# A fused attention and Fourier-mixing kernel: mirrored rows of batch 2 computed on chip again, the last batch's turned in DRAM in four column pieces

## The chip, the core and the metric

The kernel runs on one core of one Trainium2 chip. The core has five engines with instruction queues of their own: TensorE (PE in the profile, its weight loads PEld), VectorE (DVE), ScalarE (ACT), GpSimd (POOL) and SyncE (SP). SP and ACT also issue most of the DMA transfers. The metric is the device time of one execution in microseconds (us); lower is better. Times of engines below are counted from the start of the profiled span.

## What is computed

The inputs are q, k, v of shape (4 batches, 8 heads, 768 positions, 64) and two matrices of an MLP. Attention looks at 8 global positions and at a local band of 96, with a bias per head; its output x has shape (4, 768, 512). Then follows a Fourier mixing and an MLP:

```
scores = q k^T / sqrt(D) + bias, masked; a = softmax(scores); x = a v, as (B, 768, 512)
X     = fft(fft(x, axis=1), axis=2)
u     = x + real(X)
un    = (u - mean(u)) / sqrt(var(u) + 1e-6)
out   = u + max(un @ w_ch1, 0) @ w_ch2
```

For real x the real part of the two-dimensional transform is symmetric: the value at row -s, column -d equals the value at row s, column d. Rows s = 6m+1 and 6m+2 therefore hold, in reverse order of rows and of columns, what is needed for rows 6m+5 and 6m+4.

## The kernel before, in words

Work is written for one batch at a time: attention (scores `score`, P·V `av`), then `bounce`, `fold_s`, `fold_d`, `y_unit`, `mirror`, `u_unit`, `nt_unit`, and then the MLP (`ph_unit` for the first matrix, `pg_unit` and, for the last pair, `pg_last` for the second). The 768 rows of a batch are six residue classes 6m+r of 128 rows. They are handled as three pairs of classes; pair number c = 3b + pr runs from 0 to 11 over the whole kernel.

- `bounce` writes the attention output X to a DRAM buffer (xd, L737) and reads it back by residue class (xr; L751 and L752, and L760 for the classes 4 and 5). From batch 1 on it issues all this on ACT.
- `fold_s`, `fold_d` and `y_unit` make the first transform by foldings on DVE and matmuls on PE (py, L934 to L941). ACT or DVE empty PSUM into Y (tile zy, L955 and L957). Only 14 of the 24 combinations of row and column class are computed; the others are mirror images.
- `u_unit` makes the second transform of a pair by 16 matmuls (pu, L1032); `u_rows` adds x on DVE (L1072).
- `nt_unit` normalises and transposes. For b > 1 the transposes are DMA transposes on SP (L1121); each call of the function `xbar` there issues two, one for each class of the pair.
- `ph_unit` (L1171, emptied by ACT L1177 or DVE L1178) and `pg_unit` (L1194, the sum with u on DVE L1205, the store L1216) finish a pair. The output tile ob has two buffers. The last half pair is made in two column halves, with the add at L1243 and the store at L1246.

There are two ways to the mirrored classes 4 and 5. `FLIP(b)` chooses; it is true for batches 2 and 3.

1. Without FLIP (batches 0 and 1), `mirror` makes reversed copies of Y (r0 for one tile, and rn, L993, for four more in a tile of tag ww), and the pairs are (1,2), (0,3), (4,5): three u units.
2. With FLIP, only r0 is done. The pair (1,2) and the pair (5,4) share one PSUM bank of one u unit: the second is read backwards in columns (`turned` in `u_rows`). Its rows are in reverse order too. So x of these classes is turned in DRAM: two DRAM-to-DRAM transfers into xe (L757), then one read into SBUF (xr from xe, L764). And its output is stored to a staging buffer in DRAM (oe, L1214) and from there, turned, into the output (`back`, L1221). The turning transfers run over 16 column pieces, then rows, then the elements of a piece. This makes two u units a batch.

The order of instructions comes from a planner, `Plan`. Every piece of work has an assumed cost and the tokens it needs. Matmuls stand in four streams (MIX, ATT, PH, PG), of which the first ready one is taken; the rest of the engines get what is ready earliest. Nothing at run time reorders an engine's queue. Work that gets its engine late holds all behind it on that engine. The planner's figures for DMA (for example 1.35 us of ACT for all of `rd`) are constants in the code.

A buffer is reused when its users are done: `buf(tag, i, ..., users)` sets the number of users and `pl.used` counts them. Tag ww has one buffer.

The main loop, at its end, for one batch (the branch for FLIP ends with `continue`):

```python
mirror(b)
if FLIP(b):
    nt_unit(b, 0)
    nt_unit(b, 1)
    u_unit(b, 2)
    nt_unit(b, 2)
    continue
if b:
    u_unit(b, 0)
u_unit(b, 1)
for rows in ((0,), (1,)):
    nt_unit(b, 0, rows)
u_unit(b, 2)
nt_unit(b, 1)
nt_unit(b, 2)
```

Of the kernel before, what the change touches and what calls it, by code (L numbers as in the profile page):

```python
# [9 lines left out]
FP16 = mybir.dt.float16  # L10
# [4 lines left out]
P = 128  # L15
# [139 lines left out]
def mm_us(n, k=1):  # L155
    return k * max(n / 2400.0 + 0.0025, 0.029)


def act(n):
    return 0.19 + n / 1200.0  # L160
# [15 lines left out]
def kernel(  # L176
# [11 lines left out]
    nc = tc.nc  # L188
    B, H, S, Dh = q.shape
# [92 lines left out]
    def free(tag, i):  # L282
        i -= NBUF[tag]
        return [("free", tag, i)] if i >= 0 else []

    def buf(tag, i, shape, dtype, users):
        pl.users(("free", tag, i), users)
        return wk.tile(shape, dtype, tag=tag, name=f"{tag}_{i}", bufs=NBUF[tag])
# [18 lines left out]
    v16 = [kon.tile([P, NS, H, 66], FP16, tag=f"v16{i}", name=f"v16{i}") for i in range(2)]  # L307
# [181 lines left out]
    def BANKS(b):  # L489
        return ("xx", "C", "D") if b == 0 else ("xx",)  # L490
# [234 lines left out]
    T = {}  # L725

    def bounce(b):

        on, eng = ("ACT", nc.scalar) if b else ("SP", nc.sync)
        for half in range(2):  # L730
            def wr(half=half):
                if half == 0:
                    XD[b] = dr.tile([S, Dm], FP16, tag="xd", name=f"xd_{b}", bufs=2)
                c = slice(half * 256, half * 256 + 256)
                rows = XD[b][:, c].rearrange("(j m t) d -> t m j d", t=2, m=64)
                for t in range(2):
                    eng.dma_start(rows[t], X[b][64 * t:64 * t + 64, :, c])  # L737
            pl.later([(on, 1.2, wr)], [("x", b, hp, jp) for hp in (2 * half, 2 * half + 1) for jp in range(NP)] + [("xwi", b)][:half], 0.0,
                     [("xw", b, half)], [("free", "x", b)], lat=4.4 if b == 1 else 1.6, dma=1.2,
                     then=lambda t, half=half: half or pl.tok.__setitem__(("xwi", b), pl.t[on]))  # L740

        XE = {}

        def issued(t):
            pl.tok[("xri", b)] = pl.t[on]
            pl.tok[("xe", b)] = t + 4.0

        def rd():
            rows = XD[b].rearrange("(m r) d -> m r d", r=6)
            XR[b] = [buf(f"xr{i}", b, [P, 2, DP if i == 1 and FLIP(b) else Dm], FP16, 1) for i in range(3)]  # L750
            eng.dma_start(XR[b][0], rows[:, 1:3])  # L751
            eng.dma_start(XR[b][2 if FLIP(b) else 1], rows[:, 0:4:3])  # L752
            if FLIP(b):

                XE[0] = dr.tile([2, P, Dm], FP16, tag="xe", name=f"xe_{b}", bufs=2)
                for a in range(2):
                    eng.dma_start(XE[0][a].rearrange("m (h d) -> h m d", h=16),  # L757
                                  rows[::-1, 4 + a].rearrange("m (h d) -> h m d", h=16))
            else:
                eng.dma_start(XR[b][2], rows[:, 4:6])  # L760
        pl.later([(on, 1.35, rd)], [("xw", b, 0), ("xw", b, 1)] + free("xr0", b) + free("xr1", b) + free("xr2", b), 0.0,
                 [("xr", b)], lat=2.0 if b else 0.6, dma=2.2, then=issued)
        if FLIP(b):
            pl.later([(on, 0.5, lambda: eng.dma_start(XR[b][1][:, :, 0:Dm], XE[0].rearrange("a p d -> p a d")))], [("xe", b)], 0.0,  # L764
                     [("xrb", b)], lat=2.0, dma=0.7)
# [73 lines left out]
    def NA(b):  # L839
        return (0, 2, 1, 1)[b]  # L840

    def IW(b, n):

        return (0, 2, 6, 8)[b] + n
# [125 lines left out]
    def mirror(b):  # L970

        def r0(cp):
            rev = buf("rev0", b, [P, 2, 2, P], FP16, 2)
            src = T[("y", b)][:, 4]
            cp(rev[:, 0, :, 0:1], src[:, 0, :, 0:1])
            cp(rev[:, 0, :, 1:P], src[:, 0, :, P - 1:0:-1])
            cp(rev[:, 1], src[:, 1, :, ::-1])
            Y[(b, 0, 3, "r")], Y[(b, 3, 3, "r")] = rev[:, 0], rev[:, 1]
        pl.later([("ACT", 1.0, lambda: r0(nc.scalar.copy)), ("DVE", 0.8, lambda: r0(V.tensor_copy))] if b else
                 [("POOL", 1.0, lambda: r0(nc.gpsimd.tensor_copy))], [("y", b, 0, 3), ("y", b, 3, 3)] + free("rev0", b), 0.0,  # L980
                 [("y", b, 0, 3, "r"), ("y", b, 3, 3, "r")], [("free", "zy", 2 * b + 1)])
        if FLIP(b):
            return

        def rn(n, on):
            if n == 0:
                T[("rev", b)] = buf("ww", IW(b, NA(b) + 1), [P, 4, 2, 2, P], FP16, 1)
            rev = T[("rev", b)]
            d, y = rev[:, n], T[("y", b)][:, n, :, :, ::-1]
            if on == "ACT":  # L990
                A(d, y, AF.Copy)
            else:
                (V if on == "DVE" else nc.gpsimd).tensor_copy(d, y)  # L993
            for a in range(2):
                Y[(b,) + YG[n // 2][2 * (n % 2) + a] + ("r",)] = rev[:, n, a]
        for n in range(4):
            ys = YG[n // 2][2 * (n % 2):2 * (n % 2) + 2]
            pl.later([("ACT", act(512), lambda n=n: rn(n, "ACT")), ("DVE", 0.7, lambda n=n: rn(n, "DVE")) if b else ("POOL", 1.0, lambda n=n: rn(n, "POOL"))],
                     [("y", b) + y for y in ys] + free("ww", IW(b, NA(b) + 1)) + [("rv", b, n - 1)][:n], 0.0,
                     [("y", b) + y + ("r",) for y in ys] + [("rv", b, n)],  # L1000
                     [("free", "zy", 2 * b + 1)] if n == 3 else [])

    def ysrc(rs, rd):
        if (rs, rd) in POS:
            return rs, rd, False
        return (6 - rs) % 6, 4 - rd if rd else 0, True
# [1 line left out]


    def FLIP(b):  # L1010
        return b > 1

    def PAIRS(b):
        return ((1, 2), (5, 4), (0, 3)) if FLIP(b) else ((1, 2), (0, 3), (4, 5))
# [7 lines left out]
    def u_unit(b, pr):  # L1022
        src = {(a, rd): ysrc(rs, rd) for a, rs in enumerate(PAIRS(b)[pr]) for rd in range(4)}
        needs = [("y", b, r2, d2) + (("r",) if m else ()) for r2, d2, m in src.values()]

        def run(start, ring):
            pu = bank(ring, f"pu_{NP * b + pr}")
            for (a, rd), (r2, d2, mir) in src.items():
                yy = Y[(b, r2, d2, "r") if mir else (b, r2, d2)]
                o = pu[:, a, rd * P:(rd + 1) * P]  # L1030
                for x in range(2):
                    nc.tensor.matmul(o, yy[:, x, :], t2_sb[:, rd, (0 if x == 0 else (2 if mir else 1)), :],  # L1032
                                     start=(x == 0), stop=(x == 1))
            e = pl.pe(mm_us(P, 16), start)
            if pr < 2 or FLIP(b):
                pl.used(("free", "zy", 2 * b + 1), e)
            if PAIRS(b)[pr] == (0, 3):
                for _ in range(2):
                    pl.used(("free", "rev0", b), e)
                if not FLIP(b):  # L1040
                    for _ in range(3):
                        pl.used(("free", "zy", 2 * b + 1), e)
            if PAIRS(b)[pr] == (4, 5):
                pl.used(("free", "ww", IW(b, NA(b) + 1)), e)
            if FLIP(b) and pr == 0:
                u_rows(NP * b, pu, e, None)
                u_rows(NP * b + 1, pu, e, ring)
            else:
                u_rows(NP * b + pr, pu, e, ring)
        MIX.append((needs + ([("h", 0, 1)] if b == 0 and pr == 2 else []), BANKS(b) if pr < 1 else ("xx",), run))  # L1050
# [133 lines left out]
    def pg_unit(c, t, part):  # L1184
        b, pr = divmod(c, NP)
# [3 lines left out]
        def run(start, ring):  # L1189
# [11 lines left out]
            cell = {}  # L1201
# [7 lines left out]
            eng = nc.scalar if c < 6 else nc.sync  # L1209
# [8 lines left out]

            def back():
                o = out[b].rearrange("(m r) d -> m r d", r=6)[::-1, rs, :]  # L1220
                eng.dma_start(o.rearrange("m (h d) -> h m d", h=16), cell[1].rearrange("m (h d) -> h m d", h=16))  # L1221
            if FLIP(b) and pr == 1:
                pl.later([("ACT" if c < 6 else "SP", 0.45, back)], [("st", i)], 0.0, [], lat=1.6, dma=1.0)
        PG.append((needs, ("pg",) if part == 0 else None, run))
# [29 lines left out]
    with tc.manual_schedule():  # L1254
# [79 lines left out]
        for b in range(B):  # L1334
# [39 lines left out]
            for g in (0, 1, 2, 3):  # L1374
# [4 lines left out]
                if FLIP(b) and g == 1:  # L1379
# [4 lines that stand above are left out]
# [58 lines left out]
```

## Time and profile before

| | |
|---|---|
| five runs, us | 268.36, 269.26, 271.26, 271.51, 274.1; median 271.26 |
| profiled execution, us | 271.26 |
| its span from first to last instruction, us | 269.5 |
| mean granted clock of TensorE | 0.994 |
| DMA packets, of these under 512 bytes | 100302, 62388 |
| DMA moved | 42.81 MB, 159 GB/s over the span |
| xe from xd: issues, KB each, median us to landing | 4, 128.0, 5.4 |
| oe from ob | 4, 256.0, 2.0 |
| out from oe (turned store) | 4, 256.0, 3.5 |
| DMA transposes of un (L1121): issues, us to landing | 12, 2.5 |

How to read the profile: an engine's busy time is the time its instructions ran; idle time is put down to the work that ended it. A name with q (ACTq, SPq) is the engine's instruction queue at work on something that is not counted as busy, such as issuing a transfer; "issue" is waiting that the profile can't attribute. DMA share is the mean busy share of the 16 DMA engines in a window; records of packets overlap, so it can exceed 1. The granted clock is the share of TensorE's full clock that it was given.

### The profile page before, as it was taken

Reading aid. Unit: us, or ns where it says so; the run is one execution under the profiler, and the core shown is the slowest. Engines: PE = TensorE matmul, PEld = TensorE weight load, DVE = VectorE, ACT = ScalarE, POOL = GpSimd, SP = SyncE. Lnnn points to the kernel's source line nnn. Section 1 sums busy time; section 2 is a strip of 40 time slices with the busy share of each in tenths; the row PEclk is TensorE's granted clock in tenths of the full one; section 3 lists DMA queues with packets and bytes.
Section 4 is the critical chain, followed back from the end, with each engine's and each line's share of the span. In section 5 each row is a group of like instructions: output and inputs, shape, how many; then the busy total and the mean of one; then the engine's idle time right before and its main releaser. Section 6 shows DMA issues by size and latency. Waiting matters only on the chain.

```text
span 269.5 us, 5931 instructions
## 1 busy us (share of the span) xinstructions
PE 255.2 (95%) x2378; PEld 172.2 (64%) x2378; DVE 179.3 (67%) x367; ACT 135.7 (50%) x231; POOL 67.9 (25%) x120
## 2 busy tenths in 40 slices
PE   7789898999999999999998799999999999999993
PEld 3445587887765466877964456677676676666453
DVE  4676978867789998968796478779956614211221
ACT  2877366878633758686331337782353353524000
POOL 1573624597111452534031301011000110100000
PEclk9999999999999999999999799999999999999999
DMA  7999979999989979997299932022572442411144
GB/s 217 291 295 301 201 197 227 219 262 208 214 203 297 314 231 206 208 170 114 61 182 198 235 86 71 4 41 58 129 126 61 120 96 60 98 39 41 39 117 117
DMA packets 100302, 42.81 MB, mean 159 GB/s; under 512 B 62388, under 2 KB 96180, under 8 KB 100148
## 3 DMA queue, kind: packets, MB, share of 16 engines
q1 hardware_dynamic: 79332, 29.86, 48.6%
q10 hardware_dynamic: 16720, 8.39, 12.7%
q0 software_dynamic: 4224, 4.19, 9.7%
q8 instruction: 18, 0.29, 0.5%
q14 instruction: 8, 0.07, 0.1%
HBM read 34.05 MB, written 11.01 MB: 167 GB/s over the span
## 4 chain that ended last, share of the span: by engine, by line
PE 75%; DMA 9%; DVE 6%; ACTq 3%; SPq 2%; POOL 1%; issue 1%; ACT 1%; DVEq 0%; POOLq 0%
PE ph L1171 29%; PE pg L1194 27%; PE sc L569 4%; PE pu L1032 3%; PE pav L698 3%; DMA xe<-xd 2%; DMA qs<-in_q_dram 2%; PE pt L531 2%; SPq L405 2%; DMA qkT<-qk 2%; PE py L934 2%; DVE x L718 2%; PE py L938 2%; DMA out_dram<-ob 1%; DMA xd<-x 1%
## 5 line engine op out<-in xcount | busy, mean ns | idle before, releaser
L1171 PE MATMUL ph<-unT,w 128*128 128x256 f16 x768 | 94.0, 273 | 0.4 <-ACT hT L1177 0.2
L1194 PE MATMUL pg<-w,hT 128*128 128x512 f16 x368 | 87.1, 382 | 0.0
L1171 PEld LDWEIGHTS <-w 128*128 128x128 f16 x768 | 72.1, 98 | 16.8 <-issue 5.3
L1177 ACT ACTIVATE hT<-ph 128x512 f16<-128x512 f32 x59 | 35.0, 596 | 51.7 <-PE ph L1171 42.2
L1194 PEld LDWEIGHTS <-hT 128*128 128x128 f16 x368 | 35.0, 98 | 36.1 <-issue 2.0
L592 ACT ACTIVATE er<-sc 128x992 f16<-128x992 f32 (+2 forms) x42 | 38.0, 924 | 9.7 <-PE sc L569 6.0
L1205 DVE SCALAR_TENSOR_TENSOR ob<-pg,sm,u 128x512 f32<-128x512 f32 x23 | 17.2, 748 | 38.2 <-PE pg L1194 32.9
L1178 DVE TENSOR_SCALAR hT<-ph 128x512 f16<-128x512 f32 x37 | 25.4, 688 | 16.6 <-PE ph L1171 16.2
L607 DVE TENSOR_TENSOR ex<-er,mk 128x992 f16<-128x992 f16 (+2 forms) x42 | 28.2, 689 | 2.3 <-ACT er L592 2.2
L423 POOL CAST qk<-qs 128x768 f16<-128x768 f32 x21 | 19.1, 914 | 25.0 <-issue 12.2
L1110 POOL TENSOR_SCALAR sm<-sm 128x2 f32<-128x2 f32 x12 | 3.0, 249 | 82.6 <-ACT un L1103 82.5
L718 DVE TENSOR_TENSOR x<-pav,rc 128x512 f16<-128x512 f32 (+1 forms) x27 | 17.1, 632 | 0.9
L1072 DVE SCALAR_TENSOR_TENSOR u<-pu,xr 128x512 f32<-128x512 f32 x24 | 15.7, 688 | 2.3 <-PE pu L1032 1.8
L1103 ACT ACTIVATE un<-un 128x512 f16<-128x512 f16 x24 | 15.0, 624 | 4.4 <-DMA unT<-un 3.4
L569 PE MATMUL sc<-qkT 64*128 64x256 f16 (+1 forms) x192 | 16.1, 261 | 0.7 <-ACT v L470 0.5
L698 PEld LDWEIGHTS <-ex 128*128 128x128 f16 x352 | 15.1, 97 | 2.0 <-DVE rc L717 0.4
L698 PE MATMUL pav<-v,ex 128*128 128x65 f16 x352 | 16.3, 193 | 0.0
L955 ACT ACTIVATE zy<-py 128x512 f16<-128x512 f32 x17 | 9.8, 594 | 12.4 <-DVE eA L873 5.2
L479 POOL CAST v<-vs 128x768 f16<-128x768 f32 x12 | 11.6, 977 | 12.1 <-DMA vs<-in_v_dram 11.9
L512 POOL COPY kG<-qkT 64x8 f16<-64x8 f16 x32 | 8.0, 251 | 25.5 <-DVE qkT L540 18.7
L330 PE MATMUL fill<-eg 128*128 128x512 f16 x46 | 12.6, 419 | 1.4 <-DVE eg L1268 1.2
L569 PEld LDWEIGHTS <-qkT 64*128 64x128 f16 x192 | 6.3, 94 | 11.7 <-issue 9.0
(120 smaller groups left out, 285.5 us busy)
## 6 DMA issues: line engine op xcount, KB each, us to landing
vs<-in_v_dram SPq DMA_DIRECT2D x24, 192.0 KB, 5.5
w<-in_moe_w_ch_dram POOLq DMA_DIRECT2D x8, 512.0 KB, 9.7
qs<-in_q_dram SPq DMA_DIRECT2D x9, 384.0 KB, 6.5
qs<-in_k_dram SPq DMA_DIRECT2D x9, 384.0 KB, 5.9
out_dram<-ob ACTq DMA_DIRECT2D x12, 256.0 KB, 4.0
xd<-x ACTq DMA_DIRECT2D x12, 192.0 KB, 3.5
xr<-xd ACTq DMA_DIRECT2D x7, 256.0 KB, 4.9
out_dram<-ob SPq DMA_DIRECT2D x7, 256.0 KB, 2.1
```

Of the source, the lines that this page charges most:

```text
L423: nc.gpsimd.tensor_copy(d, s)
L569: nc.tensor.matmul(pa[:, s, c0:c0 + cw], TT[n][lo:lo + 64, 1, i * P:(i + 1) * P], TT[n][lo:lo + 64, 0, i * P:i * P + cw], start=(not inps) ...
L592: A(mine(), cut(pa), AF.Exp, 0.0, 0.125)
L607: VT(o, mine(), m, op=ALU.mult)
L698: nc.tensor.matmul(po[:, jj, hh * 65:(hh + 1) * 65], lhsT, v16[b % 2][:, i, h, 0:65], start=(jp == 0 and a == 0), stop=(a == len(ops) - 1) ...
L718: VT(X[b][:, 2 * jp:2 * jp + 2, first * Dh:(first + nh) * Dh].rearrange("p j (h d) -> p j h d", d=Dh), pv[:, :, :, 0:Dh], rc.to_broadcast( ...
L1072: V.scalar_tensor_tensor(o.rearrange("p (n r) -> p n r", r=4), i, 1.0, xx.rearrange("p (n r) -> p n r", r=4), op0=ALU.mult, op1=ALU.add, a ...
L1171: nc.tensor.matmul(ph[:, a * CH:(a + 1) * CH], w1[:, d, jb * P:(jb + 1) * P], UNT[c][:, d, :], start=(d == 0), stop=(d == ND - 1))
L1177: pl.later([("ACT", act(512), lambda: A(dst, ph, AF.Relu)), ("DVE", dve(512), lambda: V.tensor_scalar_max(dst, ph, 0.0))], [], e, [("h", c ...
L1178: ("DVE", dve(512), lambda: V.tensor_scalar_max(dst, ph, 0.0))],
L1194: nc.tensor.matmul(pg, HT[c][:, jb, t * P:(t + 1) * P], w2[:, jb, :], start=(jb == 0), stop=(jb == NJ - 1))
L1205: V.scalar_tensor_tensor(cell[0], pg, MV[c][:, t, 3:4], UT[c][:, t, 0:Dm], op0=ALU.mult, op1=ALU.add)
```

## The change

`FLIP` becomes true for the last batch alone, so batch 2 takes the first way: four more reversed copies of Y, the pairs (1,2), (0,3), (4,5), three u units, a plain read of x for classes 4 and 5, plain stores, and the other branch of the main loop, with its two calls of `nt_unit` for the first pair. Its reversed copies lie in v16[0], the tile of V of batches 0 and 2, once batch 2's P·V is done (`avdone`). In the last batch the turning transfers run over 4 column pieces in place of 16 (256 bytes at a time in place of 64 for xe, 512 in place of 128 for the output), and xe is issued on SP in place of ACT.

```diff
                 for a in range(2):
-                    eng.dma_start(XE[0][a].rearrange("m (h d) -> h m d", h=16),
-                                  rows[::-1, 4 + a].rearrange("m (h d) -> h m d", h=16))
+                    nc.sync.dma_start(XE[0][a].rearrange("m (h d) -> h m d", h=4),
+                                  rows[::-1, 4 + a].rearrange("m (h d) -> h m d", h=4))
...
             if n == 0:
-                T[("rev", b)] = buf("ww", IW(b, NA(b) + 1), [P, 4, 2, 2, P], FP16, 1)
+                if b < 2:
+                    T[("rev", b)] = buf("ww", IW(b, NA(b) + 1), [P, 4, 2, 2, P], FP16, 1)
+                else:
+                    T[("rev", b)] = v16[0].rearrange("p j h d -> p (j h d)")[:, 0:16 * P].rearrange(
+                        "p (n a c m) -> p n a c m", n=4, a=2, c=2)
...
-                     [("y", b) + y for y in ys] + free("ww", IW(b, NA(b) + 1)) + [("rv", b, n - 1)][:n], 0.0,
+                     [("y", b) + y for y in ys] + (free("ww", IW(b, NA(b) + 1)) if b < 2 else [("avdone", b)]) + [("rv", b, n - 1)][:n], 0.0,
...
     def FLIP(b):
-        return b > 1
+        return b == B - 1
...
-            if PAIRS(b)[pr] == (4, 5):
+            if PAIRS(b)[pr] == (4, 5) and b < 2:
                 pl.used(("free", "ww", IW(b, NA(b) + 1)), e)
...
-                eng.dma_start(o.rearrange("m (h d) -> h m d", h=16), cell[1].rearrange("m (h d) -> h m d", h=16))
+                eng.dma_start(o.rearrange("m (h d) -> h m d", h=4), cell[1].rearrange("m (h d) -> h m d", h=4))
```

## The prediction

> **What bounds the kernel now.** I read the page's busy shares first, then who waited for whom on PE, then the chain of waits and ACT's timeline around PE's one long hole, then the end of the span.
>
> ```profile
> PE 255.2 (95%) x2378; PEld 172.2 (64%) x2378; DVE 179.3 (67%) x367; ACT 135.7 (50%) x231; POOL 67.9 (25%) x120
> ...
> PE py L938 <- ACT zy L955: 2.9, 1, 2.9
> ```
>
> TensorE is the bound. After the start it has one long hole, in batch 2: a Y matmul waits 2.9 us for ACT to empty a PSUM bank. ACT itself was not computing:
>
> ```profile
> 140.00 4.71 ACTq L757 DMA_DIRECT2D xe<-xd  x2
> 144.76 1.08 ACT L1177 ACTIVATE hT<-ph 128x512 f16<-128x512 f32 x2 [5.70 <-PE py L938]
> 146.75 2.06 ACTq L1216 DMA_DIRECT2D out_dram<-ob  x1
> 148.93 1.09 ACT L955 ACTIVATE zy<-py 128x512 f16<-128x512 f32 x2 [3.09 <-issue]
> ```
>
> ACT was issuing transfers in order: the two turnings of x in DRAM (xe, L757) hold it to 144.7, and the store behind them (L1216) to 148.8; the chain of waits runs through the first xe (140.00, 6.66 us) into L1216. Only then do the evacuations (zy, L955) run. The hole also costs clock (columns: window, length, PE busy, granted clock, DMA share, GB/s):
>
> ```profile
> 147.00:148.00 1.00, 0.14 (x1) 1.00 1.41 169
> 148.00:149.00 1.00, 0.00 (x0) 1.00 1.43 168
> 149.00:150.00 1.00, 0.00 (x0) 1.00 1.43 162
> 150.00:151.00 1.00, 0.93 (x9) 1.00 1.29 274
> 151.00:152.00 1.00, 1.00 (x7) 0.55 1.14 362
> 152.00:153.00 1.00, 1.00 (x5) 0.50 1.20 375
> 153.00:154.00 1.00, 1.00 (x6) 0.50 0.53 93
> 154.00:155.00 1.00, 1.00 (x16) 0.75 0.54 184
> ```
>
> The missing clock is 0.45+0.50+0.50+0.25 = 1.70 us of full-speed work. From 155 to 265.4 PE is all but gapless. The end:
>
> ```profile
> 257.89 0.57 SPq L1221 DMA_DIRECT2D out_dram<-oe  x1
> ...
> 259.27 0.44 SPq L1214 DMA_DIRECT2D oe<-ob  x1
> ...
> 261.97 0.56 SPq L1221 DMA_DIRECT2D out_dram<-oe  x1
> 262.00 0.75 DVE L1205 SCALAR_TENSOR_TENSOR ob<-pg,sm,u 128x512 f32<-128x512 f32 x1 [2.76 <-PE pg L1194]
> 262.78 0.96 SPq L1216 DMA_DIRECT2D out_dram<-ob  x1
> ...
> 266.17 0.48 DVE L1243 SCALAR_TENSOR_TENSOR ob<-pg,sm,u 128x256 f32<-128x256 f32 x1 [2.00 <-DMA out_dram<-ob]
> ```
>
> SP's order is turned store, its staging store, turned store, plain store. The last add waits 2.00 us for that plain store to free its buffer. So the last batch's turned stores lie ahead of the end.
>
> The sum is made against the profiled execution: span 269.5, time 271.26 (1.8 us around the span), which is also the median of the five runs.
>
> **Batch 2 no longer turned: what goes.** Two xe transfers and the read back (L764) leave ACT; two staging and two turned stores (215.9 to 230.1) leave SP, where PE was gapless, worth nothing. One plain read (L760) comes on ACT, 0.6 us after L752 as in batch 1 (94.3 there). ACT is then free by about 140.6, and the store's data are ready at 144.03 (add at 143.29, 0.74). The first Y bank is full at 144.55; PE went on 1.14 us after ACT began evacuating (148.93 to 150.07), so it can go on at 145.7, and PE has matmuls until 147.14. The hole closes with 1.4 us to spare: -2.93, and with it the slow clock, -1.70. What is late next is nothing before the pg matmuls run out (below). If ACT stays held beyond 146.0, each further microsecond is one of PE again; both ends: -4.63 and 0.
>
> The clock gate: the row shows half clock for about 3.4 us after an idle of 2.93 us. The Trainium skill (TensorE: Matmul & The Clock Gate, Part 1: The HAM clock gate) says the clock is halved after at least one idle window of about 3.4 us. By that rule this hole would have cost no clock and the sum would be 1.70 us higher; the row shows that it did.
>
> **Batch 2: what comes.** A third u unit: 16 matmuls at L1032, 0.89 us on PE (156.05 to 156.94), all on the path: +0.89. Four mirrored copies of Y on DVE or ACT, 0.28 us on DVE in batch 1 (L993, 128x512 f16): 1.1 us. DVE stood still 3.7 us at 145.8 to 149.6, and PE has pg matmuls meanwhile: 0; without that cover 1.1. They lie in v16[0], which the last P·V of batch 2 (ended 132.7) had released: no wait. The two small turning copies on DVE go: 0.
>
> **Batch 2's transposes.** The main loop's other branch calls nt_unit twice for the first pair, and on the xbar path each call issues both transposes. SP gets two more, 1.2 us each, and the pair's unT lands about 2.5 us later. Queued behind them on SP are the next pair's transposes, and ph of the first pair waits. In before the first u matmuls end at 155.2, the two transposes are issued at 157.3 to 159.9 and land 2.5 us after issue, about 161.1. With the hole gone u ends near 150.5, the doubled unT is there near 159. From 150.5 PE still has 56 pg matmuls (192 in six pairs, 136 done), 12 us, and two u units, 1.8 us: to about 164. Cost 0; without cover 2.5.
>
> **Batch 3: xe moved to SP.** ACT's two issues (194.48 to 197.36) go; behind them hT, waiting 3.47 us, held PE for 0.2 (ph L1171) and then 0.3 (py L938): -0.5, at least 0. SP has nothing from 177 to 205.9; behind xe stand the next transposes, whose data come at 205.9. The read back on ACT waits for xe, issued at 202.94; behind it hT (204.69) and un. On four engines the two are 64 KB per engine: at 18.6 GB/s per engine (first window below) 3.5 us, at 10 (128-byte packets) 6.5; with xd landed at 193.4 and 1.4 us from issue to first packet (as at 257.89) xe lands between 198.3 and 201.3, before 202.94; DVE's turned add comes at 210.57. Cost 0; without cover about 1.5.
>
> **Batch 3: turned stores in 4 pieces.** Each is 256 KB: 2,048 packets of 128 bytes become 512 of 512. The trace shows no transfer cut in four. One end: spread over 16 engines, 262,144 bytes at the 298 GB/s of the 512-byte loads (5 to 9 us: 2,272 packets, 1.19 MB), 0.9 us. Other end: one piece per engine, so four engines carry 64 KB each while twelve idle. Rows, DMA share and GB/s last:
>
> ```profile
> 8.00:9.00 1.00, 1.00 1.20 288
> ...
> 186.00:187.00 1.00, 0.00 (x0) 1.00 0.98 230
> ...
> 259.60:259.90 0.30, 1.00 1.28 202
> ...
> 261.10:261.40 0.30, 1.00 0.80 301
> ```
>
> At 298/16 = 18.6 GB/s 64 KB take 3.5 us; at the 512-byte bounce writes' 230/16 = 14.4, 4.6; at the 2 KB stores' 301/0.80/16 = 23.5, 2.8. Now a turned store moves in 1.6 us (DMA starts at 259.3; the staging store's higher rate has taken over by 260.9). I take one piece per engine, because now 16 pieces keep 16 engines busy and the piece is the outermost loop in both patterns; and 3.5 us, the row with the same packet size read from DRAM. So +1.9 per turned store. It counts twice, if each engine serves the queue in order: the staging store (259.27) ends behind the first turned store, SP waits for it before issuing the second (261.97), and the plain store comes behind that, with the last add waiting on it: +3.8. Ends: one piece per engine +2.4 (2.8 us) to +6.0 (4.6 us), or half if the staging store overtakes; spread over 16, -0.7, since the last add can't begin before PE's last matmuls end at 265.4 instead of 266.17.
>
> The Trainium skill speaks against this edit (DMA: Bandwidth & Descriptors, Rules for kernel authors, "Use all 16 engines"): an outermost dimension below 16 confines a transfer to that many engines. By it the one-piece end holds, the sum is the one below; without it the other end would give 266.3. No run here shows it yet.
>
> **Sum.** 271.26 - 2.93 - 1.70 - 0.50 + 0.89 + 3.8 = 270.8: what is won in batch 2 is given back at the end.
>
> **The rivals.** *A, the forecast, 0.54:* hole gone, tail longer: 270.8; own range 269.0 (+2.0) to 273.0 (+6.0).
> *B, the pieces are spread over all engines, 0.18:* 271.26 - 5.13 + 0.89 - 0.7 = 266.3. For it: smaller packet counts are cheaper (202 GB/s against 288). Against it: four pieces can't be dealt evenly to 16 unless they are cut again.
> *C, another wait takes the hole's place, 0.16, slower:* ACT is held in batch 2 by the third read or the store. For it: the second xe began at 143.87, 3.2 us after the first was issued, with ACT doing nothing, so a DMA issue can wait for something other than its data; loads keep DMA share at 1.1 to 1.5 there. Against: in batch 1 the three reads and the store go out from 93.3 to 95.1 with no hole. If the hole stays whole: 270.8 + 4.63 = 275.4; it decides once hole and clock together cost over 3.2 us, 1.5 us of hole where the clock loss stays 1.70.
> *D, tail worse, 0.08, slower:* four engines at less than 13 GB/s each, 5.1 us per turned store, +7: 274.0 and more. For it: reads and writes both strided in DRAM. Against: 128-byte packets on the same path go at 10 to 13 GB/s per engine already, and larger ones were faster in every row.
> The last 0.04: neither gain nor loss of size.
>
> **How the numbers follow.** About 1% is what a measurement of this kernel can tell from no change (five runs: 268.36 to 274.1). Under 268.55 lie B and a few hundredths of A: 0.21. Over 273.97 lie C (most) and D: 0.22. Within: 0.57. The range from 266.0 to 274.8 leaves out the lower part of B and most of C's full hole.
>
> **What would show it.** Right: PE's wait for zy L955 in batch 2 gone, granted clock 1.0 throughout; 16 more matmuls at L1032; four turned stores become two, landing 5 us or more instead of 3.5; at the end DMA share near 0.25 for some 3 us, and the last add's wait longer by about 4. Wrong: a turned store landing under 3 us (B); ACT's evacuation still late near 149 (C); PE idle before ph of batch 2's first pair, which would make the doubled transposes count; ACT waiting at L764 for xe in batch 3.

## The result and the profile after

| | before | after |
|---|---|---|
| median of the runs, us | 271.72 (80 runs, 268.36 to 277.2) | 272.83 (43 runs, 271.34 to 277.0) |
| ratio of after to before, 95% interval | 1 | 1.0077 [1.006, 1.0095] |
| profiled execution / its span, us | 271.26 / 269.5 | 272.35 / 270.4 |
| PE's last matmul ends, us | 265.40 | 261.77 |
| from there to the end of the span, us | 4.1 | 8.6 |

The changed kernel is slower by 0.0077 x 271.7 = 2.1 us (the medians of all runs differ by 1.1). The forecast was 0.2% faster; the measured change goes the other way, by more than its interval. The profiled executions of after_back16 and before_store_pool were disturbed ones, 1 to 2% above the medians of their kernels, so their spans are not compared.

Line numbers are those of each run's own kernel. From the mirrored copies on, after's are 5 higher than before's: L1221 is the turned store in before and the plain store in after, where the turned store is L1226.

The two profiled executions split the difference cleanly. PE ends 3.6 us earlier, and what follows PE's end is 4.5 us longer: -3.6 + 4.5 = +0.9, against +1.1 in their times.

From the page of after, the busy times; PE has 16 matmuls more, the third u unit:

```profile
PE 255.1 (94%) x2394; PEld 172.0 (64%) x2394; DVE 176.9 (65%) x362; ACT 139.5 (52%) x238; POOL 68.3 (25%) x120
```

PE's list of waits for 128 to 210 us is empty in after, where before had the 2.9 us at L938. ACT's queue at the same place (timeline of after; start, length, and in brackets the idle time ahead and what ended it):

```profile
139.35 0.53 ACTq L760 DMA_DIRECT2D xr<-xd  x1
140.71 0.60 ACT L1182 ACTIVATE hT<-ph 128x512 f16<-128x512 f32 x1 [0.98 <-PE ph L1176]
...
144.72 0.36 ACTq L1221 DMA_DIRECT2D out_dram<-ob  x1
145.67 1.08 ACT L955 ACTIVATE zy<-py 128x512 f16<-128x512 f32 x2 [3.48 <-DVE eA L873]
148.09 0.35 ACTq L1221 DMA_DIRECT2D out_dram<-ob  x1
148.73 0.60 ACT L955 ACTIVATE zy<-py 128x512 f16<-128x512 f32 x1 [1.46 <-PE py L941]
```

The plain read (L760) is out at 139.9, hT follows, and the first two Y banks are emptied from 145.67 where it was 148.93. The end of the span in the timeline of after:

```profile
254.25 0.66 SPq L1226 DMA_DIRECT2D out_dram<-oe  x1
...
255.63 0.45 SPq L1219 DMA_DIRECT2D oe<-ob  x1
258.11 3.66 PE L1240 MATMUL pg<-w,hT 128*128 128x256 f16 x32
...
260.62 0.62 SPq L1226 DMA_DIRECT2D out_dram<-oe  x1
...
261.34 1.02 SPq L1221 DMA_DIRECT2D out_dram<-ob  x1
...
266.95 0.48 DVE L1248 SCALAR_TENSOR_TENSOR ob<-pg,sm,u 128x256 f32<-128x256 f32 x1 [5.75 <-DMA out_dram<-ob]
```

PE is done at 261.77, and the last add begins at 266.95: it waited 5.75 us for the plain store (2.00 before). Followed back, the chain of waits of after runs through the stores on SP:

```profile
255.63 4.97 DMA oe<-ob
...
260.62 0.62 SPq L1226
...
261.34 5.49 DMA out_dram<-ob
```

The staging store, behind the first turned store, takes 4.97 us to land (2.7 before, from 259.27 to 261.97). The plain store, behind the second, takes 5.49 (3.27 before). The windows over the first turned store and over the end (window, length, PE busy, granted clock, DMA share, GB/s):

```profile
257.00:258.00 1.00, 1.00 (x6) 1.00 0.42 136
258.00:259.00 1.00, 1.00 (x11) 1.00 0.26 77
259.00:260.00 1.00, 1.00 (x12) 1.00 0.20 73
...
265.00:266.00 1.00, 0.00 (x0) 0.53 0.27 90
266.00:267.00 1.00, 0.00 (x0) 0.50 0.15 55
```

Shares of 0.20 to 0.27 are four engines of sixteen, which fits one piece per engine; the higher share before 258 has the staging store's packets in it. A turned store moves in 3.8 to 3.9 us (1.6 before): the 512 packets of the first one run from about 255.7 to 259.6, which is 128 on each of four engines at 30 ns. The low clock at 265 lies where PE has nothing left to do.

### The profile page after: what moved, and what is told of

Its sections match the earlier page's. It is cut to its first block, busy times and chain, and to the rows that moved or that the text cites. A ratio compares the mean times of both kernels' runs of the same rounds, so it can differ in the third digit from the quotient of the medians.

```text
span 270.4 us, 5971 instructions
## 1 busy us (share of the span) xinstructions
PE 255.1 (94%) x2394; PEld 172.0 (64%) x2394; DVE 176.9 (65%) x362; ACT 139.5 (52%) x238; POOL 68.3 (25%) x120
## 4 chain that ended last, share of the span: by engine, by line
PE 74%; DMA 11%; DVE 7%; SPq 5%; issue 1%; POOL 1%; ACT 0%; DVEq 0%; ACTq 0%; POOLq 0%
PE ph L1176 31%; PE pg L1199 26%; SPq L405 4%; PE sc L569 4%; DMA qs<-in_k_dram 3%; PE pav L698 3%; PE pu L1037 3%; DMA u<-in_v_dram 3%; DMA out_dram<-ob 2%; DMA oe<-ob 2%; DVE x L718 2%; PE py L938 1%; PE pt L531 1%; DMA xd<-x 1%; PE pav L687 1%
## 5 line engine op out<-in xcount | busy, mean ns | idle before, releaser
L1199 PE MATMUL pg<-w,hT 128*128 128x512 f16 x368 | 86.2, 379 | 0.0
L1182 ACT ACTIVATE hT<-ph 128x512 f16<-128x512 f32 x61 | 36.4, 597 | 52.0 <-PE ph L1176 51.7
L1183 DVE TENSOR_SCALAR hT<-ph 128x512 f16<-128x512 f32 x35 | 24.1, 690 | 13.9 <-PE ph L1176 13.4
L569 PE MATMUL sc<-qkT 64*128 64x256 f16 (+1 forms) x192 | 16.3, 261 | 0.8 <-ACT v L470 0.4
L330 PE MATMUL fill<-eg 128*128 128x512 f16 x46 | 13.2, 434 | 1.4 <-DVE eg L1273 1.2
L569 PEld LDWEIGHTS <-qkT 64*128 64x128 f16 x192 | 6.3, 94 | 11.8 <-issue 9.2
```

Of the source, the lines that this page charges most:

```text
L569: nc.tensor.matmul(pa[:, s, c0:c0 + cw], TT[n][lo:lo + 64, 1, i * P:(i + 1) * P], TT[n][lo:lo + 64, 0, i * P:i * P + cw], start=(not inps) ...
L1182: pl.later([("ACT", act(512), lambda: A(dst, ph, AF.Relu)), ("DVE", dve(512), lambda: V.tensor_scalar_max(dst, ph, 0.0))], [], e, [("h", c ...
L1183: ("DVE", dve(512), lambda: V.tensor_scalar_max(dst, ph, 0.0))],
L1199: nc.tensor.matmul(pg, HT[c][:, jb, t * P:(t + 1) * P], w2[:, jb, :], start=(jb == 0), stop=(jb == NJ - 1))
```

## The experiments

The theory after the result: batch 2's gain is as forecast, and the price is the turned stores, 4 to 5 us. The rivals: the price comes from something else of the change (the doubled transposes, xe on SP, a new wait in batch 2); or the hole's going is no property of the edit. Ratios are to before on the same chip, with 95% intervals.

### after_back16: the turned stores in 16 pieces again

```diff
-  eng.dma_start(o.rearrange("m (h d) -> h m d", h=4), cell[1].rearrange("m (h d) -> h m d", h=4))
+  eng.dma_start(o.rearrange("m (h d) -> h m d", h=16), cell[1].rearrange("m (h d) -> h m d", h=16))
```

> The changed kernel with its two turned stores back in 16 column pieces, nothing else undone. Theory (the gain of batch 2 is real, the loss is the last batch's turned stores on four engines): the tail after TensorE's last matmul falls from 8.6 us to about 4, so some 4.5 us under the changed kernel and 1 to 1.5% under the kernel before, near 268. Rival (the hole of batch 2 was an accident of the one profiled execution, so batch 2 gains nothing): within 0.5% of the kernel before. Rival (packet size, not engines, makes the turned store slow): no faster than the changed kernel.

Measured: 269.19 us, ratio 0.991 [0.9875, 0.9944]. Against after that is 1.0077/0.991 = 1.017, 4.6 us (3.2 to 6.0 by the ends of the two intervals): the turned stores alone, the only thing in which the two programs differ. Without them the change is faster by 0.009 x 271.4 = 2.4 us, and not by the forecast's 4.24. In its list of waits PE has one that after's profile does not have, at the u matmuls:

```profile
PE pu L1037 <- DVE zy L957: 1.7, 1, 1.7
```

The runs show one thing more. For each execution the mean granted clock over its span is on record, and it parts the 29 executions of before that ran beside this one into two groups: 15 at 0.999 or 1.0, with a median of 270.4 us, and 14 at 0.994 or below, with a median of 272.9. A loss of 1.70 us in a span of 269.5 makes 0.994. So about half of before's executions lose next to no clock and have no 1.70 us to win back. after_back16 is 1.2 us faster than the first group and 3.7 us faster than the second. No execution of before with the full clock was profiled; whether its hole is shorter is not known.

### before_back4: the four pieces put into before

The same line of before (L1221), 16 turned into 4, in both turned batches.

> The kernel before with only its turned stores cut into 4 pieces (batches 2 and 3 both; those of batch 2 lie under matmuls). Theory (four engines at the end): the last add waits some 4.5 us longer, about 276, 1.6% slower than before. Rival (the loss lies in batch 2's extra work): within 0.5% of before.

Measured: 276.66 us, ratio 1.0172 [1.0112, 1.0232], +4.7 us. The end in its timeline:

```profile
261.31 0.64 SPq L1221 DMA_DIRECT2D out_dram<-oe  x1
...
262.70 0.77 SPq L1214 DMA_DIRECT2D oe<-ob  x1
...
267.17 0.62 SPq L1221 DMA_DIRECT2D out_dram<-oe  x1
...
273.10 0.48 DVE L1243 SCALAR_TENSOR_TENSOR ob<-pg,sm,u 128x256 f32<-128x256 f32 x1 [5.34 <-DMA out_dram<-ob]
```

The same picture as after: the second turned store goes out 4.5 us after the staging store that it waits for, and the last add waits 5.34 us. So the price comes without the rest of the change too, and belongs to the pieces. The agreement of 4.7 with 4.6 is partly luck. Of the 6.9 us by which this profile's span is longer than before's, 3.4 lie ahead of PE's end (in batch 2 its hole was 3.9 us long, and the clock loss there 3.4 us), and the tail from PE's end is 3.5 us longer, where after's is 4.5.

### after_back8 and after_back32: other numbers of pieces

The line of after_back16 with 8 and with 32 in place of 16.

> The changed kernel with its turned stores in 8 pieces (256-byte packets). Theory (one piece, 128 packets, per engine, and the price of a packet grows with its size): eight engines at 18 to 20 ns a packet, about 2.5 us per turned store, 1.3 us under the four pieces' 3.9 and 0.9 over the 16 pieces' 1.6; the tail is 2.6 us under the changed kernel's, the time 0.2% under to 0.2% over the kernel before. Rival (larger packets are cheaper, the tail has another cause): faster than with 16 pieces, under 0.991 of the kernel before.

> The changed kernel with its turned stores in 32 pieces (64-byte packets). Theory: all 16 engines, but 256 packets each, at 12 to 13 ns about 3.2 us per turned store, 1.6 over the 16 pieces; twice at the end, so some 3 us over the 16-piece version, 0.2% over the kernel before. Rival (only the number of engines counts): as 16 pieces, 0.9% faster than the kernel before.

Measured: 8 pieces 270.58 us, 0.9965 [0.9929, 1.0002]; 32 pieces 272.25 us, 1.0037 [1.0001, 1.0073]. The last add in the timelines, first of 8 pieces:

```profile
264.51 0.48 DVE L1248 SCALAR_TENSOR_TENSOR ob<-pg,sm,u 128x256 f32<-128x256 f32 x1 [3.58 <-DMA out_dram<-ob]
```

And of 32:

```profile
266.74 0.48 DVE L1248 SCALAR_TENSOR_TENSOR ob<-pg,sm,u 128x256 f32<-128x256 f32 x1 [5.27 <-DMA out_dram<-ob]
```

Both times are within 0.2% of what was expected. The wait is 5.75 us with 4 pieces, 3.58 with 8, about 2.4 with 16 (2.32 to 2.48 in five profiles) and 5.27 with 32. With fewer than 16, engines stand idle (a DMA share of 0.41 to 0.52 while the turned store of 8 pieces moves alone); with 32 every engine has more and smaller packets (256 of 64 bytes). Sixteen is the least of the four for both reasons.

### only_batch2: before with FLIP for the last batch alone

after_back16, and xe as in before: 16 pieces, on ACT.

```diff
-  nc.sync.dma_start(XE[0][a].rearrange("m (h d) -> h m d", h=4),
-                rows[::-1, 4 + a].rearrange("m (h d) -> h m d", h=4))
+  eng.dma_start(XE[0][a].rearrange("m (h d) -> h m d", h=16),
+                rows[::-1, 4 + a].rearrange("m (h d) -> h m d", h=16))
```

> The kernel before with only batch 2 no longer turned; the last batch turns as before, in 16 pieces, xe on ACT. Theory: PE's hole in batch 2 and its slow clock are gone, 4.6 us less, 0.9 us of u matmuls more: about 267.6, 1.4% faster than before. Rival (the hole is an accident of one execution): 0 to 0.4% slower than before, by the added matmuls.

Measured: 269.87 us, 0.9947 [0.9907, 0.9986]: faster than before, which refutes the rival, but 2.3 us short of the forecast 267.6. xe on ACT against xe on SP (after_back16) is 1.0 us more by the ratios, with intervals that overlap: the right sign for the forecast's 0.5, and not settled. The old hole is gone, and PE has another wait in batch 2:

```profile
PE pu L1037 <- DVE zy L957: 1.8, 1, 1.8
```

ACT's timeline shows what it is:

```profile
144.90 0.34 ACTq L1221 DMA_DIRECT2D out_dram<-ob  x1
145.85 1.08 ACT L955 ACTIVATE zy<-py 128x512 f16<-128x512 f32 x2 [3.31 <-DVE eA L873]
...
150.44 0.34 ACTq L1221 DMA_DIRECT2D out_dram<-ob  x1
150.83 0.60 ACT L955 ACTIVATE zy<-py 128x512 f16<-128x512 f32 x1 [3.39 <-DMA qkT<-qk]
```

The second store of the pair goes out at 150.44 where after had 148.09, and the Y evacuation behind it at 150.83 for 148.73. The chain of waits names what the store waited for:

```profile
140.31 10.06 DMA qkT<-qk
...
150.44 0.34 ACTq L1221
...
150.83 0.60 ACT zy L955
...
151.46 0.70 DVE zy L957
...
152.21 1.05 PE pu L1037 x16
```

A DMA transpose of q and k on SP, issued at 140.3, landed 10 us later, and a store on ACT with which it shares no data waited for that landing. The compiled instruction streams show by what. A completion semaphore is a counter that a transfer raises when it has landed. The transfers of SP and ACT share eight of them (DMAHW0 to DMAHW7) in turn, and before each transfer but the first eight (147 of 155 in only_batch2) the issuing engine waits until the last user of its semaphore has landed, beside what its data need. The first and second store of this pair in ACT's stream, the same in after and only_batch2 (place in the stream, line, operation, waits):

```
148 L1221 DMACopy out_dram<-ob_2492 128x512 [waits DMAHW2_49,DVE_49]
152 L1221 DMACopy out_dram<-ob_2529 128x512 [waits DMAHW7_49,DVE_49]
```

DVE's semaphore is the data's. The count of DMAHW7 that is waited for is raised by a transpose of q and k at L505 on SP, and by the trace it was such a transpose's landing that ended the wait.

### after_back16_shift: another semaphore for the store

after_back16 with one transfer of 64 bytes more on SP behind batch 2's reads, so that the store takes another semaphore of the eight.

```diff
+  if b == 2:
+      nc.sync.dma_start(dr.tile([1, 32], FP16, tag="extra", name="extra", bufs=1), w2[0:1, 4, 0:32])
```

> The changed kernel with its turned stores in 16 pieces and one more transfer, of 64 bytes, on SP behind batch 2's reads of x; it moves each later transfer on by one of the eight completion semaphores that SP and ACT share. Theory (in batch 2 ACT's second store waits for a transpose of k on SP, only because it has the same semaphore; that holds the Y evacuations and PE's u matmuls for 1.7 to 1.8 us): the store starts when its data are there, PE no longer waits at L1037 in batch 2, some 1.8 us less than with 16 pieces alone, about 1.6% faster than before. Rival (crowded DMA makes ACT late, whatever the semaphore): as with 16 pieces alone, about 0.9% faster than before, with PE's wait still there.

Measured: 270.02 us, 0.9946 [0.9912, 0.998]; PE's wait at pu is 1.8 us still. ACT's timeline:

```profile
149.88 0.37 ACTq L1223 DMA_DIRECT2D out_dram<-ob  x1
150.30 0.60 ACT L957 ACTIVATE zy<-py 128x512 f16<-128x512 f32 x1 [3.30 <-DMA xr<-xd]
```

Now the wait is put down to the third read of x (L760), issued at 140.25, and the compiled stream agrees: with the one transfer more, the store has DMAHW0, and the count that it waits for is this read's. The special form, that the one transpose is to blame, fell, and with it the forecast of 1.8 us. What was issued near 140 lands near 150, and the store waits for whichever of these its semaphore had. DMA share is 0.98 to 1.56 in each microsecond from 140 to 152.

### after_one_nt: the first pair of batch 2 transposed once

after_back16, with the two calls of `nt_unit` made one in batch 2.

```diff
-  for rows in ((0,), (1,)):
+  for rows in ((0,), (1,)) if b < 2 else ((0, 1),):
```

> The changed kernel with its turned stores in 16 pieces and the first pair of batch 2 transposed once, not twice. Theory (PE has pg matmuls left when unT lands): nothing gained, within 0.3% of the 16-piece version, 0.9% faster than before; PE shows no wait at ph in batch 2 in either. Rival (the doubled transposes hold ph of the first pair): 1 to 2.5 us faster than the 16-piece version.

Measured: 269.09 us, 0.993 [0.9892, 0.9967], beside after_back16's 0.991 [0.9875, 0.9944]: no difference that shows, though the intervals are wide enough to hide 1 us. What settles it is the profile of after: with the transposes doubled, PE waits for nothing from 128 to 262 us.

### before_again: the program before, profiled once more

> The kernel before once more, for a second profile of it. Theory (PE's hole in batch 2 belongs to the kernel): again 2 to 4 us of PE waiting for zy in batch 2 and a granted clock near 0.994. Rival (it belongs to single executions): a hole under 1 us and a clock of 1.0.

One run, 272.47 us. PE's waits in batch 2:

```profile
PE py L938 <- ACT zy L955: 3.2, 1, 3.2
PE py L938 <- DVE zy L957: 0.6, 1, 0.6
```

The hole is in each profile with before's order of work (2.9 and 3.2 in two of before, 3.9 in before_back4), so it is not an accident of the first. But these three executions have clocks of 0.994, 0.993 and 0.983; that the clock loss belongs to every execution is not shown, and the clocks beside after_back16 speak against it.

### before_xe_sp: xe on SP in before, in both turned batches

```diff
-  eng.dma_start(XE[0][a].rearrange("m (h d) -> h m d", h=16),
+  nc.sync.dma_start(XE[0][a].rearrange("m (h d) -> h m d", h=16),
```

> The kernel before with the turning of x (xe, 16 pieces, batches 2 and 3) issued on SP in place of ACT, nothing else. Theory (ACT held by issuing xe makes the hole): the hole and the 0.5 us of batch 3 go without any extra matmuls, about 266.5, 1.8% faster than before, unless SP's transposes of batch 3's q and k, now behind xe, come late. Rival (the hole comes from the crowded DMA, whoever issues): within 0.5% of before, with ACT still late at zy in batch 2.

Measured: 273.88 us, 1.0062 [1.0022, 1.0101], slower and not the forecast 266.5: the exception that the expectation named is what came. The hole at L938 is gone, and a longer one stands in its place: PE waits 4.6 us ahead of the next batch's scores (L569).

```profile
PE sc L569 <- issue: 4.6, 1, 4.6
```

SP's timeline:

```profile
147.75 4.44 SPq L757 DMA_DIRECT2D xe<-xd  x2
152.36 3.27 SPq L505 DMA_TRANSPOSE qkT<-qk  x2
```

SP's last transposes of q and k for batch 3 now stand behind xe and go out at 152.4, and the trace has PE's 4.6 us among the waits for these transposes. The windows around (PE busy, granted clock, DMA share, GB/s):

```profile
159.00:160.00 1.00, 0.00 (x0) 1.00 0.07 14
160.00:161.00 1.00, 0.73 (x6) 1.00 0.00 0
161.00:162.00 1.00, 1.00 (x4) 0.52 0.04 12
162.00:163.00 1.00, 1.00 (x4) 0.50 0.98 299
163.00:164.00 1.00, 1.00 (x3) 0.50 0.65 122
164.00:165.00 1.00, 1.00 (x6) 0.78 0.46 92
```

The clock is lost again: 0.48 + 0.50 + 0.50 + 0.22 = 1.70 us. So moving xe to SP in batch 2 only changed who waits; in batch 3 SP has nothing behind xe that is due, and there it was free.

### after_store_pool and before_store_pool: two stores on GpSimd

If ACT's second store is what is late, then the stores of that pair (c == 3) on another queue should free the evacuations. after_back16, and before, each with:

```diff
-  eng = nc.scalar if c < 6 else nc.sync
+  eng = nc.gpsimd if c == 3 else nc.scalar if c < 6 else nc.sync
```

and the planner's engine for this piece "POOL".

> The changed kernel with its turned stores in 16 pieces and the two stores of pair 3, which ACT issues in batch 2 ahead of the Y evacuations, issued by GpSimd, whose transfers have semaphores of their own. PE's order of work is the same. Theory (ACT is held there because a store waits for an older transfer with the same semaphore, and every older transfer lands late, near 150, beside the loads of batch 3): no wait of PE at L1037 in batch 2, up to 1.8 us less than with 16 pieces alone, 0.986 of before. Rival (the evacuation is late for another reason): PE's wait at L1037 stays and the time is that of 16 pieces alone, 0.991.

> The kernel before with the two stores of pair 3 issued by GpSimd in place of ACT, nothing else. Theory (of the hole of batch 2 the part from 144.8 on belongs to the store, which waits for the first xe to land, not to the issuing of xe): the evacuations start near 145.8, PE's hole and its slow clock go, 3 to 4.6 us less than before, 0.985 of it, with batch 2 still turned. Rival (issuing xe alone holds ACT long enough): the hole shrinks by less than half, 0.993 or more.

Measured: after_store_pool 269.38 us, 0.9842 [0.9803, 0.988], 0.0158 x 272.9 = 4.3 us faster than before by the ratio, 3.5 by the medians (only six executions ran), and the fastest against before of all. PE has no wait in batch 2. ACT's timeline:

```profile
145.36 1.09 ACT L955 ACTIVATE zy<-py 128x512 f16<-128x512 f32 x2 [3.15 <-DVE eA L873]
...
148.40 1.25 ACT L955 ACTIVATE zy<-py 128x512 f16<-128x512 f32 x2 [0.92 <-PE py L941]
```

before_store_pool: 270.88 us, 0.9931 [0.9895, 0.9967], the rival's time and not the theory's 0.985. PE's waits there:

```profile
PE sc L569 <- issue: 2.2, 1, 2.2
PE py L938 <- ACT zy L955: 1.1, 1, 1.1
```

Without the store behind xe the hole falls from 2.9 to 1.1 us. The rest is xe, which held ACT from 141.76 for 6.16 us. Most of that is a wait too: the two issues themselves take 0.65 and 0.82 us, and the chain of waits has the second behind a transpose on SP:

```profile
140.01 7.07 DMA qkT<-qk
...
147.10 0.82 ACTq L757
```

In the compiled streams of before and of this run the second xe waits, by DMAHW5, for a transpose of q and k; in before the store behind it waits, by DMAHW0, for the first xe. In this profile the clock was lost behind the 2.2 us ahead of the scores, and not behind the 1.1.

## Why the prediction was right or wrong, point by point

**The hole and its clock (-2.93 - 1.70): the wait that goes was right, but the gain was taken whole, and there two steps failed.** ACT was free by 140.6 as worked out (L760 out at 139.9), the first evacuations began at 145.67 (forecast: needed by about 146.0), and no experiment with batch 2 unturned had the wait of L938 for ACT, or a slow clock in its place.

The first step that failed is "What is late next is nothing before the pg matmuls run out". Late next is the second store of the pair, on ACT ahead of Y's last evacuations. In the seven profiles with batch 2 unturned and the stores on ACT, PE waits at pu for it 0, 1.8, 1.7, 1.8, 0.6, 0.6 and 0 us (after, only_batch2, after_back16, after_back16_shift, after_back8, after_back32, after_one_nt), 0.9 in the mean. That is rival C, in part. The argument "a DMA issue can wait for something other than its data" stood in the prediction with its 3.2 us, but the forecast put it down to a rival alone and gave the likeliest case none of it. The argument against it, that the reads and the store of batch 1 go out without a hole, was read from a stretch with other loads.

The second is "and with it the slow clock, -1.70", read from one profile and taken for every execution. Of before's 29 executions beside after_back16, 15 show a clock of 0.999 or 1.0. Over all 29 the clock lost, idle tail included, is 1.24 us in the mean, and 0.50 in after_back16's 13, so by this estimate the change won about 0.7 us of clock there and not 1.70.

One reading of the profile of before was off as well. "ACT was issuing transfers in order" names the right place, but of the 4.71 us at L757 the two issues themselves take 0.62 and 0.84. The rest is a wait for the semaphore of another transfer, as before_store_pool and the compiled streams show, and so is the store's wait for the first xe, which landed at 146.66. Why the store's issue then took 2.06 us, where the next one took 0.34, is open. The hole that went and the wait that came are in the main of one kind.

**Its size by the runs.** The four terms of batches 2 and 3 add to -2.93 - 1.70 - 0.50 + 0.89 = -4.24. after_back16 gives -2.4 [-3.4, -1.5] (its ratio's interval x 271.4), 1.8 us less. By the estimates above the clock accounts for about 1.0 of this and the store's wait for about 0.9, but the division is not shown: the waits are of single profiles. With the stores out of ACT's way (after_store_pool) the gain is -4.3 [-5.4, -3.3] by the ratio and -3.5 by the medians. That points the same way, but it ran on another chip, where only 5 of before's 17 executions kept a clock of 0.999 or 1.0, so that more was to be won. In the two profiles first compared the forecast seems met: from the first P·V group of batch 2 (125.46 us before, 126.15 after) to PE's last matmul the time is 4.3 us shorter, against 4.24. That is luck of the pair: before's execution had the clock loss, and after's had no wait at pu.

**The third u unit (+0.89): right.** 16 matmuls at L1037, 0.89 us in the chain of after.

**The doubled transposes (0), the mirrored copies (0), xe on SP in batch 3 (0): right.** PE's list of waits in after, empty from 128 to 262, shows all three, and after_one_nt shows no difference for the first; the read back behind xe went out at 197.57 without a wait. The 0.50 won by taking xe off ACT is not settled (only_batch2).

**The turned stores (+3.8): the mechanism right, the size too small.** One piece per engine, four engines at work, the staging store served behind: all as written, and the delay counted twice. The mis-sized term is "3.5 us, the row with the same packet size read from DRAM". The store moved in 3.8 to 3.9 us, 64 KB in 3.85 us or 17 GB/s per engine, between the 18.6 taken and the 14.4 of the slower end. So each store adds 3.85 - 1.6 = 2.25 us and two add 4.5, which is what the tail of after shows, and the runs give 4.6 (after_back16 against after) and 4.7 (before_back4 against before, not the tail alone). The Trainium skill's rule (DMA: Bandwidth & Descriptors, Rules for kernel authors, "Use all 16 engines") is borne out here by the DMA share of 0.20 to 0.27.

**The sum.** Measured -2.4 + 4.6 = +2.2, which is the +2.1 of the runs by construction, since the 4.6 is the quotient of the two ratios. The forecast's -4.24 + 3.8 = -0.4 missed by 1.8 us in batch 2 and 0.8 in the tail, both to the same side. A forecast that balances a gain against a loss of the same size should have asked which of the two was taken at its best end: the gain was taken whole, at one of its two ends.

**The rivals.** B is refuted by the four busy engines. D asked for 5.1 us per turned store, and 3.9 came. C came in part: its wait was at most 1.8 us, short enough that no clock was lost with it, and so it stayed under the point from which it decides.

## What to carry to other kernels

Number the pieces of a transfer by the engines that they occupy before asking for larger packets: here four pieces of 512 bytes were slower than sixteen of 128 on the same path, and a slow transfer is paid again by each one that is queued behind it and waited for. When a queue is relieved of one thing, look at what else stands in it ahead of the work that was late, above all DMA issues, since they can wait for transfers with which they share no data. Take such a wait into the likeliest case as soon as the trace of before shows one, rather than leaving it to a rival. And before a loss of clock in one profile goes into a sum, look at the clocks of all executions on record.

## What the runs showed of the hardware that was not expected

- Transfers issued near 140 us, beside the loads of the next batch, landed up to 10 us later, of several kinds (a transpose 10.06 us; a read issued at 140.25 was still waited for until 149.8; in the median of 138 to 151 in after_back16_shift, transposes 9.8, loads of k 8.9, reads of x 7.8, stores 6.9, one load of q 4.8), and with completion semaphores shared between SP's and ACT's transfers this reached a store on the other queue.
- In the profiles, PE's idle times of 1.1 us (before_store_pool), 1.7 (after_back16) and 1.8 (only_batch2, after_back16_shift) cost no clock. Those of 2.2 us (before_store_pool), 2.5 (after_back16, in an earlier batch), 2.93 (before), 3.2 (before_again) and 4.6 (before_xe_sp) each came with 1.70 or 1.71 us of clock lost, and 3.9 (before_back4) with 3.4, twice as much. So the loss came in one size or twice that, and not in proportion to the idle time. Where between 1.8 and 2.2 us it begins, and whether it is the length alone that decides, was not tried.
- The time of a turned store of 256 KB follows neither the packet size nor the number of pieces alone, as far as the last add's wait shows it: this goes 5.75, 3.58, about 2.4, 5.27 us for 4, 8, 16 and 32 pieces.
